# Top-32 attention and expert layer: finding the 32nd largest score from candidates, an exact count and the next eight below

## The chip, the core and the metric

The kernel runs on one NeuronCore of a Trainium2 chip. The time is the device time of one execution in microseconds (us); lower is better. The core has a matrix engine (TensorE, PE in the profile, with its weight loads as PEld), a vector engine (VectorE, DVE), a scalar engine (ScalarE, ACT), a general-purpose engine (GpSimd, POOL) and SyncE (SP), which starts transfers between the memory of the chip (DRAM) and the on-chip buffer SBUF. TensorE writes its results to PSUM. Each engine works through its own list of instructions in order; semaphores order the engines among each other.

## The reference

Everything is float32. Batch 8, 8 heads, 576 positions, head size 64; then 8 experts with 80 places each.

```python
scores = scale * np.matmul(q, k.transpose(0, 1, 3, 2))
kth = np.partition(scores, -top_k, axis=-1)[..., -top_k:-top_k + 1]     # top_k = 32
scores = np.where(scores >= kth, scores, -1000000000.0)
scores = scores - np.max(scores, axis=-1, keepdims=True)
attn = np.exp(scores)
attn = attn / (np.sum(attn, axis=-1, keepdims=True) + 1e-09)
x = np.matmul(attn, v)              # then (B, H, S, D) -> (B*S, H*D) = (4608, 512)
...
logits = x @ w_gate                 # 8 experts: each token goes to the best one
# each expert keeps its 80 tokens with the largest gate weight
h = np.maximum(x[tok_idx] @ w1[e], 0.0)
out[tok_idx] = gate_w[tok_idx, None] * (h @ w2[e])      # all other rows are zero
```

What matters here is `kth`: for each of 8 x 8 x 576 = 36,864 rows of 576 scores the 32nd largest value has to be known exactly, because it decides which scores count.

## The kernel before

The attention works on 32 pairs of heads (four for each batch). A pair has two heads of 576 rows; rows are taken in blocks of 128, so each head has four blocks, and the last 64 rows of both heads share a ninth block. These nine blocks are the **units**; there are 288 in all. A unit is a tile of 128 rows x 576 scores.

A unit goes through these stages:

- `front` (L189, L196): TensorE multiplies q and k into PSUM, ScalarE copies the scores to the SBUF tile `s`.
- `search` (L203 to L209): VectorE finds the 32 largest values of each row, eight at a time. MAX8 gives the eight largest values; match-replace overwrites them in the row by a very low value; three such rounds follow the first MAX8. The 32nd value is the last of `top`.
- `drop` (L216 to L221): `bar` is the 32nd value times 2^90 (GpSimd). ScalarE computes Relu(bar - s * 2^90), which is 0 for a kept score and huge for all others. GpSimd adds the row's maximum and subtracts the sum from the scores: `d`.
- `turn_w` (L229, L231): TensorE transposes `d` in five pieces, ScalarE takes the exponential while it copies the result out of PSUM.
- `back` (L243, L246): TensorE multiplies the weights with v, to which a column of ones is joined, so that the sum of the weights comes out with the product.

After the last unit of a pair `norm` (L257 to L291) divides by that sum on GpSimd, writes x to DRAM and adds to the gate's logits; after two batches `gates` chooses the experts. `turn` (L163 to L165) transposes q and k of the next pair, once in nine units.

The order of all instructions is written out by hand in `step(i)`. One step issues, for VectorE, the first MAX8 of unit i between the rounds of unit i-1 in turn:

```python
for j in range(7):
    if i < NU and j % 2 == 0:
        next(searches[i])
    if 1 <= i <= NU and j % 2:
        next(searches[i - 1])
```

(each `next` is one instruction or one pair), and then `drop(i-1)`, `turn_w(i-2)`, in some steps `turn`, `front` of the units i+2 and i+3, `back(i-2)` and a stage of `norm`. Engines that are ahead simply wait for the data. After the attention the routing finds the 80 best tokens of each expert, and the experts compute (`gather`, `hidden`, `product`, `store`); that part is not changed but for its place in the file.

Of the kernel before, what the change touches and what calls it, by code (L numbers as in the profile page):

```python
# [17 lines left out]
TOP_K = 32  # L18
EPS = 1e-9
LOW = -3.0e38  # L20
BIG = 2.0 ** 90
# [3 lines left out]
def kernel(  # L25
# [32 lines left out]
    GM = 2 * NK  # L58
    FK = F // P

    const = ctx.enter_context(tc.tile_pool(name="const", bufs=1))
    wpool = ctx.enter_context(tc.tile_pool(name="wpool", bufs=4))


    xd = tc.dram_tile([N, Dm], F32, name="xd")

# [8 lines left out]
    tok_i = const.tile([P, NM], I32, name="tok_i")  # L75
    nc.gpsimd.iota(tok_i.rearrange("p (b c) -> p b c", c=NK), pattern=[[S, B], [P, NK]], base=1, channel_multiplier=1)
    tok = const.tile([P, NM], F32, name="tok")
    nc.vector.tensor_copy(tok, tok_i)
    rank_i = const.tile([P, E], I32, name="rank_i")
    nc.gpsimd.iota(rank_i, pattern=[[-1, E]], base=E, channel_multiplier=0)  # L80
    rank = const.tile([P, E], F32, name="rank")
    nc.vector.tensor_copy(rank, rank_i)
# [3 lines left out]
    def load_w(e, parts=1, pool=None):  # L86

        pool = pool or wpool
        w1_t[e] = pool.tile([P, HP, F], F32, name="w1", tag="w1")
        w2_t[e] = pool.tile([P, FK, Dm], F32, name="w2", tag="w2")  # L90
        todo = []
        for t, src, n in ((w1_t[e], moe_w1, HP), (w2_t[e], moe_w2, FK)):
            step = n // parts
            for c in range(0, n, step):
                todo.append(lambda t=t, src=src, c=c, step=step: nc.sync.dma_start(
                    t[:, c : c + step, :],
                    src[e, c * P : (c + step) * P, :].rearrange("(c p) f -> p c f", p=P)))
        return todo

    zrows = 4 * P  # L100
    slow = [lambda i=i: nc.sync.dma_start(
        out[i : i + zrows, :].rearrange("(p r) d -> p r d", p=P),
        zero.unsqueeze(1).to_broadcast([P, zrows // P, Dm])) for i in range(0, N, zrows)]
    for e in range(4):
        slow += load_w(e, 4)


    with ExitStack() as actx:
        nat = actx.enter_context(tc.tile_pool(name="nat", bufs=2))
        qkp = actx.enter_context(tc.tile_pool(name="qkp", bufs=2))  # L110
        rows = actx.enter_context(tc.tile_pool(name="rows", bufs=2))
        small = actx.enter_context(tc.tile_pool(name="small", bufs=3))
        vpool = actx.enter_context(tc.tile_pool(name="vpool", bufs=1))
        ps_s = actx.enter_context(tc.tile_pool(name="ps_s", bufs=2, space=PSUM))
        ps_w = actx.enter_context(tc.tile_pool(name="ps_w", bufs=2, space=PSUM))

        loaded, turned = {}, {}


        NV = 3  # L120
        vb = []
        for j in range(NV):
            t = vpool.tile([CK, NC, 2, D + 1], F32, name=f"vb{j}")
            nc.gpsimd.memset(t[:, :, :, D : D + 1], 1.0)
            nc.gpsimd.memset(t[:DUP, NC - 1, :, :], 0.0)
            vb.append(t)


        xTb = []
        for j in range(2):  # L130
            t = vpool.tile([P, NK * P], F32, name=f"xT{j}")
            nc.gpsimd.memset(t[:, S:], 0.0)
            xTb.append(t)

        def load(n):
            b, hp = divmod(n, HP)
            tiles = []
            for name, src in (("qn", q), ("kn", k)):
                t = nat.tile([P, NK, 2, D], F32, name=name, tag=name, bufs=1)
                for h in range(2):  # L140
                    nc.sync.dma_start(
                        t[:, 0:NF, h, :], src[b, 2 * hp + h, : NF * P, :].rearrange("(c p) d -> p c d", p=P))
                nc.sync.dma_start(
                    t[0:TL, NF, :, :], src[b, 2 * hp : 2 * hp + 2, NF * P :, :].rearrange("h p d -> p h d"))
                tiles.append(t)
            t = vb[n % NV]
            e = (NC - 1) * CK
            for h in range(2):
                nc.sync.dma_start(
                    t[:, : NC - 1, h, :D], v[b, 2 * hp + h, :e, :].rearrange("(c p) d -> p c d", p=CK))  # L150
            nc.sync.dma_start(
                t[DUP:CK, NC - 1, :, :D], v[b, 2 * hp : 2 * hp + 2, e:, :].rearrange("h p d -> p h d"))
            loaded[n] = tiles

        def turn(n):

            ts_ = []
            for i, name in enumerate(("qT", "kT")):
                src = loaded[n][i].rearrange("p c h d -> p c (h d)")
                t = qkp.tile([P, S], F32, name=name, tag=name)  # L160
                ps = ps_w.tile([P, 1024], F32, name="tp", tag="w")
# [5 lines left out]
            turned[n] = ts_  # L167


        units = []  # L170
        for n in range(NP):
            for t in range(NF):
                units += [(n, t, 0), (n, t, 1)]
            units.append((n, NF, 2))
        NU = len(units)
        UPP = NU // NP
        s_t, top_t, d_t, w_t, wT_t, xu_t, xn_t = {}, {}, {}, {}, {}, {}, {}

        def front(n, t):

            qT, kT = turned[n]
            m = P if t < NF else TL
            i = n * UPP + 2 * t
            ps = [ps_s.tile([P, 2, 512], F32, name="sp", tag="sp") for _ in range(2)]
# [6 lines left out]
            for h in range(2):  # L191
                u = i + h if t < NF else i
                if t < NF or h == 0:
                    s_t[u] = rows.tile([P, S], F32, name="s", tag="s", bufs=6)
                o = slice(off[h], off[h] + m)
                nc.scalar.copy(s_t[u][o, :].rearrange("p (j c) -> p j c", j=2), ps[h][o, :, :HS])  # L196

        def search(i):

            s = s_t[i]  # L200
            top = top_t[i] = small.tile([P, TOP_K // 8, 8], F32, name="top", tag="top")
            scr = rows.tile([P, S], F32, name="scr", tag="scr")
            nc.vector.max(out=top[:, 0, :], in_=s)  # L203
            yield
            for r in range(1, TOP_K // 8):
                nc.vector.match_replace(out=scr, in_to_replace=top[:, r - 1, :], in_values=s if r == 1 else scr,  # L206
                                        imm_value=LOW)
                yield
                nc.vector.max(out=top[:, r, :], in_=scr)  # L209
                yield  # L210

        def drop(i):

            s, top = s_t.pop(i), top_t.pop(i)
            bar = small.tile([P, 1], F32, name="bar", tag="bar")
            nc.gpsimd.tensor_scalar(bar, top[:, TOP_K // 8 - 1, 7:8], BIG, None, op0=Alu.mult)  # L216
            low = rows.tile([P, S], F32, name="low", tag="low")
            nc.scalar.activation(low, s, Act.Relu, bias=bar[:, 0:1], scale=-BIG)  # L218
            nc.gpsimd.tensor_scalar(low, low, top[:, 0, 0:1], 1.0, op0=Alu.add, op1=Alu.mult)  # L219
            d_t[i] = rows.tile([P, S], F32, name="d", tag="d")  # L220
            nc.gpsimd.tensor_tensor(out=d_t[i], in0=s, in1=low, op=Alu.subtract)  # L221

        def turn_w(i):

            dd = d_t.pop(i)
            w_t[i] = ps_w.tile([P, 1024], F32, name="pw", tag="w")
            for c in range(NC):
                k0 = c * CK if c < NC - 1 else S - CK
                nc.tensor.transpose(w_t[i][:CK, c * P : (c + 1) * P], dd[:, k0 : k0 + CK], ident)  # L229
            wT_t[i] = rows.tile([CK, NC, P], F32, name="wT", tag="wT")  # L230
            nc.scalar.activation(wT_t[i].rearrange("p c r -> p (c r)"), w_t[i][:CK, : NC * P], Act.Exp, scale=scale)  # L231

        def back(i):
            n, t, h = units[i]
            wT, pw = wT_t.pop(i), w_t.pop(i)
            if t == 0 and h == 0:
                xu_t[n] = rows.tile([P, NK, 2, D + 1], F32, name="xu", tag="xu")
            xu = xu_t[n]
# [3 lines left out]
            for c, (j, hh, r, p) in order:  # L242
                nc.tensor.matmul(pw[p : p + TL, o + j * (D + 1) : o + (j + 1) * (D + 1)], lhsT=wT[:, c, r : r + TL],  # L243
                                 rhs=vb[n % NV][:, c, hh, :], start=(c == 0), stop=(c == NC - 1))
# [5 lines left out]
        def norm(n):  # L250

            xu = xu_t.pop(n)
            xn_t[n] = rows.tile([P, NK, 2, D], F32, name="xn", tag="xn", bufs=1)
            parts = ((slice(0, P), slice(0, NF)), (slice(0, TL), slice(NF, NK)))
            z = small.tile([P, NK, 2], F32, name="z", tag="z")
# [6 lines left out]
            for p, cs in parts:  # L262
                nc.gpsimd.tensor_tensor(out=xn_t[n][p, cs, :, :], in0=xu[p, cs, :, :D], op=Alu.mult,  # L263
                                        in1=z[p, cs, :].unsqueeze(3).to_broadcast([p.stop, cs.stop - cs.start, 2, D]))
            b, hp = divmod(n, HP)
            xn = xn_t.pop(n).rearrange("p c h d -> p c (h d)")
            cols = slice(hp * P, (hp + 1) * P)
            nc.sync.dma_start(xd[b * S : b * S + NF * P, cols].rearrange("(c p) d -> p c d", p=P), xn[:, :NF, :])
            nc.sync.dma_start(xd[b * S + NF * P : (b + 1) * S, cols], xn[:TL, NF, :])
            yield  # L270
            yield
            ps = ps_w.tile([P, 1024], F32, name="tp", tag="w")
# [3 lines left out]
            xT = xTb[n % 2]  # L276
            nc.scalar.copy(xT[:, :S], ps[:, :S])
            yield
            ps = ps_w.tile([P, 1024], F32, name="tp", tag="w")
# [3 lines left out]
            if b % 2 == 0 and hp == 0:  # L283
                lg_t[b // 2] = small.tile([P, 2, NK, E], F32, name="lg", tag="lg", bufs=2)
            lg = lg_t[b // 2][:, b % 2]
            if hp == 0:
                nc.scalar.copy(lg, lp)
            else:
                part = small.tile([P, NK, E], F32, name="part", tag="part", bufs=2)
                nc.scalar.copy(part, lp)  # L290
                nc.gpsimd.tensor_tensor(out=lg, in0=lg, in1=part, op=Alu.add)  # L291
            if (n + 1) % (2 * HP) == 0:
                yield
                yield from gates(b // 2)

        lg_t = {}

        def gates(g):

# [289 lines left out]
```

## Time and profile before

| | |
|---|---|
| time, median of 3 runs | 1612.83 us (1612.36 to 1612.85) |
| span of the profiled run | 1611.3 us |
| VectorE busy | 1459.1 us (91%) |
| TensorE matmul busy | 1126.3 us (70%) |
| GpSimd busy | 770.0 us (48%) |
| ScalarE busy | 710.4 us (44%) |
| mean TensorE clock | 0.739 of full speed |
| first search begins, last search ends | 11.34 us, 1431.85 us |

A row of the page's groups has the line and engine, the operation, output <- input with partitions x elements and how often it ran; then the busy time of the group and the mean duration of one in ns; then how long its engine had been idle just before such instructions, and what ended most of that idle time. A row of the timeline has start, duration, engine, line and the same names. The durations of neighbours on one engine can overlap: the pace of an engine is read from the distance of the starts.

### The profile page before, as it was taken

What the parts mean: (1) busy time and instruction counts of PE and PEld (TensorE: products, weight loads), DVE (VectorE), ACT (ScalarE), POOL (GpSimd) and SP (SyncE); (2) the same over time, 40 slices, a digit from 0 to 9 for tenths busy, and PEclk for the clock granted to TensorE, in tenths of its full rate; (3) what the DMA queues carried; (4) which work ended last, traced back from release to release, by engine and by line L of the source; (5) the groups of instructions that cost most, each with busy time, mean ns of one, the idle gap of its engine ahead of it and who ended that gap; (6) DMA issues with size and microseconds to landing.
All of it is one profiled execution on the core that took longest, in us unless ns stands there. A gap on an engine that the chain in (4) does not pass through costs nothing. (4 is left out here: it accounts for less than half of the span.)

```text
span 1611.3 us, 30682 instructions
## 1 busy us (share of the span) xinstructions
PE 1126.3 (70%) x11501; PEld 836.2 (52%) x11501; DVE 1459.1 (91%) x3075; ACT 710.4 (44%) x1341; POOL 770.0 (48%) x1071
## 2 busy tenths in 40 slices
PE   4777777676677767767766777677667777760688
PEld 3455545555455555555555555555555555540687
DVE  7999999999999999999999999999999999968311
ACT  3444454444454444545444544545454455430011
POOL 3455555555554555555555555555555555540111
PEclk9777777777777777777677777777777777765699
DMA  3022222221112222222111121111111000011280
GB/s 93 1 82 83 82 83 56 56 57 40 39 35 57 56 56 57 56 56 57 47 47 35 42 56 30 31 30 31 31 31 31 24 19 19 9 52 68 74 288 23
DMA packets 153267, 85.35 MB, mean 53 GB/s; under 512 B 117024, under 2 KB 135456, under 8 KB 153120
## 3 DMA queue, kind: packets, MB, share of 16 engines
q1 hardware_dynamic: 152096, 80.78, 18.6%
q0 software_dynamic: 1024, 2.62, 0.5%
q8 instruction: 91, 1.49, 0.4%
q14 instruction: 56, 0.46, 0.1%
HBM read 63.19 MB, written 20.19 MB: 52 GB/s over the span
## 5 line engine op out<-in xcount | busy, mean ns | idle before, releaser
L209 DVE MAX8 top<-scr 128x8 f32<-128x576 f32 x864 | 620.7, 746 | 0.1
L243 PE MATMUL pw<-vb,wT 116*64 116x65 f32 x5760 | 314.0, 262 | 267.8 <-ACT wT L231 265.3
L243 PEld LDWEIGHTS pw<-vb,wT 116*64 116x64 f32 x5760 | 267.5, 170 | 408.3 <-ACT wT L231 385.3
L206 DVE MATCH_REPLACE8 scr<-top,scr 128x576 f32<-128x576 f32 x576 | 428.1, 743 | 0.0
L221 POOL TENSOR_TENSOR d<-s,low 128x576 f32<-128x576 f32 x288 | 406.3, 1411 | 24.0
L218 ACT ACTIVATE low<-s,bar 128x576 f32<-128x576 f32 x288 | 223.6, 776 | 402.3 <-POOL bar L216 402.3
L229 PE MATMUL pw<-ident,d 128*116 128x128 f32 x1440 | 305.2, 362 | 108.2 <-POOL d L221 103.8
L219 POOL TENSOR_SCALAR low<-low,top 128x576 f32<-128x576 f32 x288 | 214.7, 745 | 313.8 <-ACT low L218 293.0
L189 PE MATMUL sp<-kT,qT 64*128 64x288 f32 (+1 forms) x1280 | 295.4, 593 | 1.4 <-ACT kT L165 0.7
L229 PEld LDWEIGHTS pw<-ident,d 128*116 128x116 f32 x1440 | 215.1, 179 | 147.0 <-POOL d L221 141.7
L203 DVE MAX8 top<-s 128x8 f32<-128x576 f32 x288 | 216.5, 752 | 28.1 <-ACT s L196 28.1
L196 ACT COPY s<-sp 128x576 f32<-128x576 f32 (+1 forms) x320 | 191.2, 640 | 73.7 <-PE sp L189 72.6
L216 POOL TENSOR_SCALAR bar<-top 128x1 f32<-128x1 f32 x288 | 61.4, 213 | 327.0 <-DVE top L209 323.3
L206 DVE MATCH_REPLACE8 scr<-top,s 128x576 f32<-128x576 f32 x288 | 214.0, 743 | 0.0
L231 ACT ACTIVATE wT<-pw 116x640 f32<-116x640 f32 x288 | 197.5, 686 | 8.6 <-PE pw L229 8.5
L189 PEld LDWEIGHTS sp<-kT,qT 64*128 64x128 f32 (+1 forms) x1280 | 152.4, 247 | 69.8 <-issue 48.7
L246 ACT COPY xu<-pw 128x65 f32<-128x65 f32 x256 | 56.2, 219 | 120.9 <-PE pw L243 114.4
L163 PE MATMUL tp<-ident,kn 128*128 128x128 f32 x128 | 33.4, 411 | 37.1 <-ACT qT L165 36.5
L533 DVE TENSOR_SCALAR y<-yx,a 80x512 f32<-80x512 f32 x8 | 6.0, 747 | 44.2 <-PE yx L531 44.2
L206 DVE MATCH_VALUE_LOAD scr<-top,scr 128x8 f32 x576 | 44.8, 78 | 0.1
L534 POOL DMA_INDIRECT out_dram<-y,idx_s x8 | 7.4, 929 | 78.3 <-DVE y L533 78.3
L263 POOL TENSOR_TENSOR xn<-xu,z 128x512 f32<-128x512 f32 x64 | 44.6, 719 | 0.1
(147 smaller groups left out, 660.0 us busy)
## 6 DMA issues: line engine op xcount, KB each, us to landing
w<-in_moe_w_dram SPq DMA_DIRECT2D x32, 512.0 KB
w<-in_moe_w_dram SPq DMA_DIRECT2D x8, 2048.0 KB
out_dram<-zero SPq DMA_DIRECT2D x9, 1024.0 KB
qn<-in_q_dram SPq DMA_DIRECT2D x64, 128.0 KB
kn<-in_k_dram SPq DMA_DIRECT2D x64, 128.0 KB
xd<-xn SPq DMA_DIRECT2D x32, 256.0 KB
vb<-in_v_dram SPq DMA_DIRECT2D x64, 116.0 KB
vb<-in_v_dram SPq DMA_DIRECT2D x32, 56.0 KB
```

The costliest lines, as they stand in the source:

```text
L189: nc.tensor.matmul(ps[h][off[h] : off[h] + m, j, :HS], lhsT=qT[d, t * P : t * P + m], rhs=kT[d, j * HS : (j + 1) * HS], start=True, stop=True)
L196: nc.scalar.copy(s_t[u][o, :].rearrange("p (j c) -> p j c", j=2), ps[h][o, :, :HS])
L203: nc.vector.max(out=top[:, 0, :], in_=s)
L206: nc.vector.match_replace(out=scr, in_to_replace=top[:, r - 1, :], in_values=s if r == 1 else scr, imm_value=LOW)
L209: nc.vector.max(out=top[:, r, :], in_=scr)
L216: nc.gpsimd.tensor_scalar(bar, top[:, TOP_K // 8 - 1, 7:8], BIG, None, op0=Alu.mult)
L218: nc.scalar.activation(low, s, Act.Relu, bias=bar[:, 0:1], scale=-BIG)
L219: nc.gpsimd.tensor_scalar(low, low, top[:, 0, 0:1], 1.0, op0=Alu.add, op1=Alu.mult)
L221: nc.gpsimd.tensor_tensor(out=d_t[i], in0=s, in1=low, op=Alu.subtract)
L229: nc.tensor.transpose(w_t[i][:CK, c * P : (c + 1) * P], dd[:, k0 : k0 + CK], ident)
L231: nc.scalar.activation(wT_t[i].rearrange("p c r -> p (c r)"), w_t[i][:CK, : NC * P], Act.Exp, scale=scale)
L243: nc.tensor.matmul(pw[p : p + TL, o + j * (D + 1) : o + (j + 1) * (D + 1)], lhsT=wT[:, c, r : r + TL], rhs=vb[n % NV][:, c, hh, :], start= ...
```

## The change

The full search is replaced by a shorter one that doesn't always succeed, with a count that tells whether it did:

1. `parts`: the row is cut into six parts of 96 scores, and MAX8 gives the eight largest of each: 48 candidates.
2. `search`: MAX8 and match-replace over the 48 candidates give their 24th largest value, `w9[7]`.
3. One instruction over the whole row makes `y = (s >= w9[7]) - s` and sums it into `cnt`. The scores have been scaled by 2^-48 when they were copied from PSUM, so that in float32 the sum is exactly the number of scores that are at least `w9[7]`, and `y` is 1 for those and -s for the others.
4. `turn_sign`: GpSimd negates `y`; MAX8 over it gives the next eight values below, `w9[8:]`.
5. `pick`: with the count between 24 and 32, the 32nd largest value is one of the nine values `w9[7:]`; a comparison of the count with the numbers 32 to 24, multiplied by these values and summed, picks it.

A row whose count is not between 24 and 32 makes the result useless. `judge` looks for such a row in all counts after the attention, and at the end of the program a branch on every engine runs the whole kernel again with the full search if there is one. `bar` is gone, since the scaled scores can be subtracted first and multiplied by 2^100 afterwards. A unit now takes part in three steps of the search: `drop` comes at i-3, `turn_w` and `back` at i-4, and there are 7 tiles `s` in place of 6.

```diff
-                nc.scalar.copy(s_t[u][o, :].rearrange("p (j c) -> p j c", j=2), ps[h][o, :, :HS])
+                nc.scalar.activation(self.s[u][o, :].rearrange("p (j c) -> p j c", j=2), ps[h][o, :, :HS], Act.Copy,
+                                     scale=TINY)
...
-            nc.vector.max(out=top[:, 0, :], in_=s)
-            yield
-            for r in range(1, TOP_K // 8):
-                nc.vector.match_replace(out=scr, in_to_replace=top[:, r - 1, :], in_values=s if r == 1 else scr,
-                                        imm_value=LOW)
-                yield
-                nc.vector.max(out=top[:, r, :], in_=scr)
-                yield
+        def parts(self, i):
...
+            for j in range(NG):
+                nc.vector.max(out=cand[:, j, :], in_=s[:, j * S // NG : (j + 1) * S // NG])
+                yield
...
+        def search(self, i):
...
+            for r in range(G0 // 8):
+                dst = top[:, r, :] if r < G0 // 8 - 1 else w9[:, :8]
+                nc.vector.max(out=dst, in_=cand)
+                yield
+                if r < G0 // 8 - 1:
+                    nc.vector.match_replace(out=cand, in_to_replace=dst, in_values=cand, imm_value=LOW)
+                    yield
+            y = self.y[i] = self.rows.tile([P, S], F32, name="y", tag="y")
+            nc.vector.scalar_tensor_tensor(out=y, in0=s, scalar=w9[:, 7:8], in1=s, op0=Alu.is_ge, op1=Alu.subtract,
+                                           accum_out=self.cnt[:, i : i + 1])
+            yield
+            nc.vector.max(out=w9[:, 8:], in_=self.y.pop(i))
+            yield
...
+            nc.vector.scalar_tensor_tensor(out=pick, in0=past, scalar=self.cnt[:, i : i + 1], in1=w9[:, 7:], accum_out=self.thr[i],
+                                           op0=Alu.is_equal, op1=Alu.mult)
+            yield
...
+        def turn_sign(self, i):
+            y = self.y[i]
+            nc.gpsimd.tensor_scalar(y, y, -1.0, 0.0, op0=Alu.mult, op1=Alu.add)
...
-            nc.gpsimd.tensor_scalar(bar, top[:, TOP_K // 8 - 1, 7:8], BIG, None, op0=Alu.mult)
...
-            nc.scalar.activation(low, s, Act.Relu, bias=bar[:, 0:1], scale=-BIG)
-            nc.gpsimd.tensor_scalar(low, low, top[:, 0, 0:1], 1.0, op0=Alu.add, op1=Alu.mult)
+            nc.scalar.activation(low, s, Act.Relu, bias=thr[:, 0:1], scale=-1.0)
+            nc.gpsimd.tensor_scalar(low, low, BIG, top[:, 0, 0:1], op0=Alu.mult, op1=Alu.add)
...
+                for c in "GbGcGdGeGgGfah":
+                    if c == "G":
+                        if i < NU:
+                            next(first[i])
+                    elif c == "a":
+                        if i < NU:
+                            next(first[i], None)
+                            second[i] = self.search(i)
+                            next(second[i])
+                    elif i - (2 if c in "gh" else 1) in second:
+                        next(second[i - (2 if c in "gh" else 1)])
+                if 0 <= i - 3 < NU:
+                    self.drop(i - 3)
+                if 0 <= i - 1 < NU:
+                    self.turn_sign(i - 1)
+                if 0 <= i - 4 < NU:
+                    self.turn_w(i - 4)
...
+            att.run(slow)
+            att.judge()
+        finish(wpool)
+    with tc.If(nc.values_load(bad[0:1, 0:1]) > 0):
+        for dma in clear():
+            dma()
```

In the string `GbGcGdGeGgGfah`, which is the order on VectorE within a step, `G` is a part of unit i; `a` to `e` are the three MAX8 and two match-replaces over the candidates (`a` of unit i, `b` to `e` of unit i-1); `f` is the count of unit i-1; `g` is the MAX8 of `y` and `h` the pick, both of unit i-2.

## The prediction, as it was put on record

> **What bounds the kernel now.** I read the page's busy shares first, then its groups of instructions, then a stretch of the timeline from mid-run.
>
> ```profile
> PE 1126.3 (70%) x11501; PEld 836.2 (52%) x11501; DVE 1459.1 (91%) x3075; ACT 710.4 (44%) x1341; POOL 770.0 (48%) x1071
> ...
> L209 DVE MAX8 top<-scr 128x8 f32<-128x576 f32 x864 | 620.7, 746 | 0.1
> ...
> L221 POOL TENSOR_TENSOR d<-s,low 128x576 f32<-128x576 f32 x288 | 406.3, 1411 | 24.0
> L218 ACT ACTIVATE low<-s,bar 128x576 f32<-128x576 f32 x288 | 223.6, 776 | 402.3 <-POOL bar L216 402.3
> ...
> L219 POOL TENSOR_SCALAR low<-low,top 128x576 f32<-128x576 f32 x288 | 214.7, 745 | 313.8 <-ACT low L218 293.0
> ```
>
> DVE is full and idles 0.1 us in front of its largest group; the 402 us in which ScalarE waits come from DVE through `bar`. So the search sets the pace. The timeline of DVE gives that pace:
>
> ```profile
> 700.28 0.08 DVE L206 MATCH_VALUE_LOAD scr<-top,scr 128x8 f32 x1
> 700.34 0.75 DVE L206 MATCH_REPLACE8 scr<-top,scr 128x576 f32<-128x576 f32 x1
> 701.00 0.75 DVE L203 MAX8 top<-s 128x8 f32<-128x576 f32 x1
> 701.66 0.75 DVE L209 MAX8 top<-scr 128x8 f32<-128x576 f32 x1
> ...
> 705.10 0.08 DVE L206 MATCH_VALUE_LOAD scr<-top,scr 128x8 f32 x1
> ```
>
> From 700.28 to 705.10 is one unit: 4.82 us. Starts are 0.66 us apart although each instruction lasts 0.75, so independent neighbours overlap. 576 elements in 0.66 us and 8 elements in 0.065 us fit a fixed 0.06 us plus one element per 1.04 ns. 288 units at 4.82 us are 1388 us; the first search starts at 11.34 us and the last ends at 1431.85 us. The remaining 179.5 us (last weighting, routing, experts) are outside the search.
>
> [...] The search of before has one input everywhere, so only the four gatings touch this. Two of them show it:
>
> ```profile
> 770.43 0.24 DVE L312 TENSOR_TENSOR oh<-oh,mx 128x80 f32<-128x80 f32 x1
> 770.47 0.82 POOL L219 TENSOR_SCALAR low<-low,top 128x576 f32<-128x576 f32 x1 [0.91 <-ACT low L218]
> ```
>
> POOL's instruction lasts 0.82 us in place of its 0.745 median, because an 80-element two-input DVE instruction (83 ns of elements) began 0.04 us earlier. The trace agrees for POOL as the loser; DVE as the loser it doesn't show. [...] L309 (80 fp32 elements) lasts 234 ns beside 241 ns of a tensor-tensor of that size. It has no accumulator, though, so I keep half rate for the range. [...] the same five transposes take 0.76 or 1.32 us, mean clock 0.73.
>
> **The change, part by part.**
>
> DVE, per unit. Removed: 4 MAX8 and 3 match-replaces of 576, 3 value loads: 4.82 us. Added, by the law above: six MAX8 of 96 at 0.16 = 0.96; three of 48 at 0.11 = 0.33; two match-replaces of 48 with loads at 0.175 = 0.35; the count (scalar-tensor-tensor of 576) 0.66; MAX8 of 576 0.66; the pick of 9 elements 0.07. Both accumulating instructions may carry a separate accumulator read, which no row of before shows: between 0 and 0.2 us each; I take a value load's 0.065. Sum 3.16 us. Dependent neighbours are kept apart by another unit's part: 0.27 us from start to start where a 48-element result takes about 0.24, so no stall. DVE falls by 1.66 us, 478 us over 288 units. I don't expect all of it, since other engines close in.
>
> POOL, per unit. Added: the sign turn of 128x576, a tensor-scalar like L219: 0.745 busy, 0.83 from start to start. Removed: `bar` (0.21). `low` (0.83) and `d` (1.37 start to start) stay. The normalisation per head pair, L257, L263 and L291, is 0.48 + 1.44 + 0.20 = 2.1 us, or 0.24 per unit. POOL's own work is 0.83 + 0.83 + 1.37 + 0.24 = 3.27 us: above DVE.
>
> The lock. The count reads two SBUF tensors, and POOL is now nearly always reading SBUF. Take the count's start as 0. It and its read end at 0.725, the next unit's first MAX8 at 0.835, the pick's threshold lands at 1.0 (a tiny DVE instruction, L465, lasts 172 ns). ScalarE's Relu follows after 0.03 and takes 0.78: 1.81. `low` starts 0.09 later, at 1.90, `d` at 2.73, and ends at 4.14. The sign turn ran in between, 0.73 to 1.5. DVE meanwhile issues 5 parts (0.80), 2 replaces (0.35), 2 small MAX8 (0.22), the MAX8 of `y` (0.66) and a sixth part (0.16) and wants its next count at 3.16, when `d` holds the port since 2.73. It waits until 4.14: **pitch 4.15 us**, DVE idle for 1 us. Queued behind the count on DVE are the pick, whose threshold Relu and then POOL wait for, so the loop closes on itself. If a delay lets the count slip in between `low` and `d`, POOL runs without gaps: 0.83 + 0.83 + 1.37 and some 0.62 in which the count blocks it, 3.65, plus 0.24: **pitch 3.89 us**. Both states are possible, the normalisation steps push into the second.
>
> The step that also transposes q and k. On TensorE it takes 8.3 us (688.41 to 696.67), and ScalarE does the copies behind it before the next Relu. Before, that cost DVE 0.9 us per head pair (L203's 28.1 us), because DVE waits for nothing else. Now DVE's MAX8 of `y` waits for the sign turn, which queues behind `low` and `d`, which wait for that Relu. The Relu comes 2 to 4 us late, of which about 1 us is slack: 1 to 3 us in nine units, 0.1 to 0.35 each. I add 0.2 to 3.89 and nothing to 4.15, which has idle time on DVE and POOL to catch up: pitch 4.1 us.
>
> TensorE, the same work: 140.8 us busy in 200 us, about 30.7 per head pair, with some 7 us of waits for the exponential, is 37.7 us per nine units, or 4.2 each, at clock 0.73. That is no slack, but at a shorter pitch it is busier and the clock should rise: at 0.8 it is 3.9.
>
> At no cost: copies out of PSUM that scale (the same pass over 576 elements on ScalarE, which has 2.5 us of work per unit); s in 7 buffers; `judge`, a few DVE instructions, beside the drain of the last units; two steps more of pipeline, one of them chained, 2.7 us from last count to last pick. The branch at the end: a load of `bad` and a jump on each engine, partly beside the landing of the last scatter: 1 to 5 us, I take 2. The second copy of the kernel doesn't run: with the seeded inputs in float32 the count lies between 24 and 32 in all 36,864 rows (34,596 at 24, one at 32).
>
> Sum: first count at about 15.5 us (11.34, one step, half the next), 287 pitches, 2.7, 179.5, 2: 200 + 287 x 4.1 = **1377 us**.
>
> **The rivals.**
> 1. No lock on DVE's side: the count slips by. POOL 3.27 and TensorE at a warmer clock 3.6 set the pitch; at 3.5, 200 + 1005 = 1205 us. For it: before shows no DVE instruction held up. Against: POOL was.
> 2. TensorE and ScalarE bound: the clock stays near 0.7, the transposing step adds its full 0.35 to 4.15: 4.5, 1492 us. For it: 4.2 us of TensorE chain. Against: the clock's rise with activity.
> 3. The count at half rate (0.6 us more, all in the loop): 4.75, 1563 us.
> 4. Slower than before: half rate and the transposing step's 0.35 together, 5.1, 1664 us; or a row counted over 32 on the chip, which runs everything again, far above 2000 us.
>
> **How the numbers follow.** Forecast (pitch 3.9 to 4.3, 1320 to 1434 us) 0.55; no lock 0.18, spread over 1150 to 1260; TensorE 0.15; half rate 0.08; slower 0.04. The range 1200 to 1510 leaves out about a third of the no-lock case, half rate and slower: 0.18. Faster: all but the last, 0.95; the same 0.01.
>
> **What would show it.** DVE's busy share falls to some 70%, with idle time or a lengthened duration at the count, overlapping `d` on POOL; MAX8 of 96 start 0.16 us apart; POOL is 75 to 85% busy; the clock rises over 0.74; the tail is still 180 us. Counts of 0.75 us that overlap `d` would refute the lock; counts that always last 1.3 us, whether or not POOL is reading, would mean half rate; TensorE without gaps in the search would mean rival 2.

## The result, and the profile after

| | before | after |
|---|---|---|
| time, median of 4 runs | 1612.84 us (1612.36 to 1614.19) | 1469.88 us (1466.17 to 1474.09) |
| ratio, 95% interval | | 0.9113 (0.9086 to 0.9141) |
| span of the profiled run | 1611.3 us | 1469.7 us |
| mean from count to count (before: from first MAX8 to first MAX8) | 4.92 us | 4.41 us |
| mean TensorE clock | 0.739 | 0.780 |

The change saves 143 us, 9%; the forecast was 236 us. The page's line of busy times:

```profile
PE 1068.7 (73%) x11502; PEld 799.3 (54%) x11502; DVE 1241.3 (84%) x5385; ACT 721.5 (49%) x1341; POOL 961.4 (65%) x1072
```

VectorE is busy for 218 us less, and POOL for 191 us more. The instruction counts are those of one pass (TensorE has 11502 instead of 11501), so the full search didn't run. But 1241 us can't all be work. By the forecast's sum VectorE needs 3.16 us per unit, 910 us for 288 units, and about 60 us in the stretch after the last pick. The rest, more than 200 us, must lie inside instructions that last longer than their work. The groups of the page show which:

```profile
L253 POOL TENSOR_TENSOR d<-s,low 128x576 f32<-128x576 f32 x288 | 459.5, 1596 | 24.0
...
L251 POOL TENSOR_SCALAR low<-low,top 128x576 f32<-128x576 f32 x288 | 223.5, 776 | 208.8 <-ACT low L250 184.7
L219 DVE SCALAR_TENSOR_TENSOR y<-s,w 128x576 f32<-128x576 f32 x288 | 347.7, 1207 | 0.0
...
L222 DVE MAX8 w<-y 128x8 f32<-128x576 f32 x288 | 213.3, 741 | 86.4 <-POOL y L232 86.4
...
L226 DVE SCALAR_TENSOR_TENSOR pick<-past,cnt,w 128x9 f32<-128x9 f32 x288 | 183.6, 638 | 0.1
```

The pick (L226) works on nine elements and has a mean of 638 ns. The count (L219) has 1207 ns, while a MAX8 over as many elements (L222) has 741. A mean can hide two populations, so the next view is the durations, as min/median/max in ns, from the rows of the trace's answers on these three lines:

```profile
L219 DVE SCALAR_TENSOR_TENSOR y<-s,w x288: 790/1209/1971, 13.8 to 1279.4; 128x576 f32<-128x576 f32 x144
...
L226 DVE SCALAR_TENSOR_TENSOR pick<-past,cnt,w x288: 201/209/1244, 17.7 to 1283.9; 128x9 f32<-128x9 f32 x144
...
L253 POOL TENSOR_TENSOR d<-s,low x288: 1397/1407/2042, 21.5 to 1289.0; 128x576 f32<-128x576 f32 x144
```

Undisturbed, the count takes 0.79 us, the pick 0.20 and `d` 1.40. Over the 288 units the counts are 120 us longer than their minimum, the picks 125 us, and `d` 55 us (each a sum of duration minus an undisturbed 0.79, 0.205 or 1.405 us). No idle time in front of an instruction shows any of this; it lies inside the instructions, and so counts as busy. It follows what runs on the other engine. The 120 counts that began while `d` ran lasted 1.08 to 1.97 us and ended 0.60 to 0.62 us after `d`; the 113 picks that did lasted 1.23 to 1.24 us and ended 0.02 to 0.04 us after it; the 100 counts and 151 picks that began while POOL ran nothing lasted at most 0.90 and 0.23 us. The other way round, the 113 `d` that began while a count ran lasted 1.77 to 2.04 us and ended 1.24 to 1.27 us after the count; the other 175 lasted at most 1.42. These waits are what is called the lock here. Some recorded texts speak of a port; the traces show the waits, not what is behind them.

The timeline shows two states. In the first, VectorE's count starts while `d` runs:

```profile
641.38 1.41 POOL L253 TENSOR_TENSOR d<-s,low 128x576 f32<-128x576 f32 x1
...
641.71 1.69 DVE L219 SCALAR_TENSOR_TENSOR y<-s,w 128x576 f32<-128x576 f32 x1
...
643.46 0.20 DVE L226 SCALAR_TENSOR_TENSOR pick<-past,cnt,w 128x9 f32<-128x9 f32 x1
643.50 0.70 POOL L232 TENSOR_SCALAR y<-y 128x576 f32<-128x576 f32 x1 [0.71 <-DVE y L219]
...
645.64 0.23 DVE L202 MAX8 cand<-s 128x8 f32<-128x96 f32 x1
645.80 1.63 DVE L219 SCALAR_TENSOR_TENSOR y<-s,w 128x576 f32<-128x576 f32 x1
```

`d` ends at 642.79, and the count, begun at 641.71, ends at 643.40: 1.08 us of wait, then a little over 0.6 us of work. The next count follows after 4.09 us. Counts wait behind `low` as well, though it reads only one SBUF tensor (here 1.21 us in place of 0.79):

```profile
632.90 0.74 POOL L251 TENSOR_SCALAR low<-low,top 128x576 f32<-128x576 f32 x1
633.04 1.21 DVE L219 SCALAR_TENSOR_TENSOR y<-s,w 128x576 f32<-128x576 f32 x1
```

Of the 169 counts that lasted over 0.9 us, 120 began while `d` ran and 49 while `low` ran; of the 135 picks over 0.3 us, 113 and 22 (these 0.49 to 0.70 us). The waits behind `low` are short: they make up 25 of the 245 us. In the second state the count is first:

```profile
658.52 0.76 DVE L222 MAX8 w<-y 128x8 f32<-128x576 f32 x1 [2.16 <-POOL y L232]
658.62 0.75 POOL L251 TENSOR_SCALAR low<-low,top 128x576 f32<-128x576 f32 x1
...
659.36 0.80 DVE L219 SCALAR_TENSOR_TENSOR y<-s,w 128x576 f32<-128x576 f32 x1
659.45 1.97 POOL L253 TENSOR_TENSOR d<-s,low 128x576 f32<-128x576 f32 x1
...
660.21 1.24 DVE L226 SCALAR_TENSOR_TENSOR pick<-past,cnt,w 128x9 f32<-128x9 f32 x1
```

Now `d` waits for the count (1.97 us in place of 1.40), and then the pick, which also reads two SBUF tensors (`past` and `w9`), waits until `d` ends at 661.42 (1.24 us in place of 0.20). The threshold comes a microsecond late for ScalarE's Relu, and VectorE has stood still behind nine elements. Sorted by state over the 277 units after the first ten, with the transposing steps apart, the distances from count to count average 4.07 us where only the count waits (116 units), 4.32 us where only the pick waits (80), 4.54 us where both wait (48), and 5.79 us in the steps that transpose q and k (31); in the other two units neither waits. Below, a step's position is the number of the unit in its pair, 0 to 8, from whose count it runs to the next count; the transposing step is position 2. The 2.16 us in brackets at 658.52 belong to such a step: VectorE idles because the sign turn is late.

### The profile page after: what moved, and what is told of

Read it like the earlier page. It is cut to its first block, busy times and chain, and to the rows that moved or that the text cites. A ratio compares the mean times of both kernels' runs of the same rounds, so it can differ in the third digit from the quotient of the medians.

```text
span 1469.7 us, 32849 instructions
## 1 busy us (share of the span) xinstructions
PE 1068.7 (73%) x11502; PEld 799.3 (54%) x11502; DVE 1241.3 (84%) x5385; ACT 721.5 (49%) x1341; POOL 961.4 (65%) x1072
## 4 chain that ended last, share of the span: by engine, by line
DVE 58%; POOL 15%; PE 14%; issue 10%; ACT 1%; DMA 0%; SPq 0%; POOLq 0%; DVEq 0%; ACTq 0%
DVE y L219 18%; DVE cand L202 12%; DVE w L222 9%; DVE pick L226 8%; POOL d L253 7%; DVE cand L216 4%; POOL low L251 4%; POOL y L232 4%; DVE top L213 3%; PE yp L603 3%; PE sp L187 2%; PE pw L275 2%; PE pw L261 2%; DVE w L213 1%; DVE top L478 1%
## 5 line engine op out<-in xcount | busy, mean ns | idle before, releaser
L202 DVE MAX8 cand<-s 128x8 f32<-128x96 f32 x1728 | 416.4, 241 | 12.9 <-ACT s L194 12.9
L219 DVE SCALAR_TENSOR_TENSOR y<-s,w 128x576 f32<-128x576 f32 x288 | 347.7, 1207 | 0.0
L250 ACT ACTIVATE low<-s,thr 128x576 f32<-128x576 f32 x288 | 223.9, 777 | 129.2 <-DVE pick L226 126.5
L222 DVE MAX8 w<-y 128x8 f32<-128x576 f32 x288 | 213.3, 741 | 86.4 <-POOL y L232 86.4
L232 POOL TENSOR_SCALAR y<-y 128x576 f32<-128x576 f32 x288 | 196.6, 683 | 98.8 <-DVE y L219 98.8
L194 ACT ACTIVATE s<-sp 128x576 f32<-128x576 f32 (+1 forms) x320 | 193.7, 648 | 129.2 <-PE sp L187 128.2
L226 DVE SCALAR_TENSOR_TENSOR pick<-past,cnt,w 128x9 f32<-128x9 f32 x288 | 183.6, 638 | 0.1
L213 DVE MAX8 top<-cand 128x8 f32<-128x48 f32 x576 | 111.5, 194 | 0.1
L216 DVE MATCH_REPLACE8 cand<-top,cand 128x48 f32<-128x48 f32 x576 | 107.2, 186 | 0.0
L213 DVE MAX8 w<-cand 128x8 f32<-128x48 f32 x288 | 53.8, 187 | 0.0
```

The source lines that it names most:

```text
L202: nc.vector.max(out=cand[:, j, :], in_=s[:, j * S // NG : (j + 1) * S // NG])
L213: nc.vector.max(out=dst, in_=cand)
L219: nc.vector.scalar_tensor_tensor(out=y, in0=s, scalar=w9[:, 7:8], in1=s, op0=Alu.is_ge, op1=Alu.subtract, accum_out=self.cnt[:, i : i + 1])
L222: nc.vector.max(out=w9[:, 8:], in_=self.y.pop(i))
L226: nc.vector.scalar_tensor_tensor(out=pick, in0=past, scalar=self.cnt[:, i : i + 1], in1=w9[:, 7:], accum_out=self.thr[i], op0=Alu.is_equal ...
L232: nc.gpsimd.tensor_scalar(y, y, -1.0, 0.0, op0=Alu.mult, op1=Alu.add)
```

## The experiments

The theory after the comparison (A) is that two separate things keep the kernel at 4.41 us: the lock between VectorE's two-input instructions and POOL, the pick included, and the transposing step, whose delay of the Relu now reaches VectorE through the sign turn. The rival (B) is that the amount of work on another engine, POOL or TensorE with ScalarE, sets the time and the waits only fill it up. In all twelve kernels the time from the first count to the last, less the waits of counts and picks and VectorE's idle time, is 3.21 to 3.32 us per unit. So a change helps by what the two kinds of waiting, in the lock and idle, lose together; several experiments below only turn one into the other. Medians of 4 runs each; the ratio is to the kernel before, run on the same chip:

| kernel | us | ratio, 95% interval |
|---|---|---|
| after | 1469.88 | 0.9086 to 0.9141 |
| pick with one SBUF input | 1444.73 | 0.8943 to 0.8997 |
| count and pick with one input | 1378.82 | 0.8532 to 0.8588 |
| q and k transposed in two steps | 1434.79 | 0.8882 to 0.8922 |
| no sign turn on POOL | 1417.94 | 0.8747 to 0.8840 |
| one input each, two steps | 1278.53 | 0.7889 to 0.7959 |
| pick before count, two steps | 1426.68 | 0.8806 to 0.8858 |
| earlier count, two steps | 1374.24 | 0.8461 to 0.8534 |
| pick with one input, two steps | 1396.06 | 0.8638 to 0.8682 |
| earlier count alone | 1414.98 | 0.8744 to 0.8835 |
| one input each, two steps, short normalisation | 1231.62 | 0.7620 to 0.7646 |
| earlier count, two steps, short normalisation | 1328.13 | 0.8217 to 0.8268 |

### The pick's second input

```diff
-            nc.vector.scalar_tensor_tensor(out=pick, in0=past, scalar=self.cnt[:, i : i + 1], in1=w9[:, 7:], accum_out=self.thr[i],
-                                           op0=Alu.is_equal, op1=Alu.mult)
+            nc.vector.tensor_scalar(pick, w9[:, 7:], self.cnt[:, i : i + 1], 0.0, op0=Alu.is_equal, op1=Alu.add,
+                                    accum_out=self.thr[i])
```

> Changed kernel, but the pick reads one SBUF tensor instead of two (a comparison of the nine values with the count, summed; the multiplication is left out, so thresholds are not the real ones). Theory A ([...] the pick alone waits 125 us in all): the pick always lasts about 0.2 us, and the time falls by 30 to 120 us, to 1350 to 1440. Theory B (TensorE and ScalarE set the pitch and VectorE's waits only fill its idle time): the picks are short, but other waits grow by as much, and the time stays within 15 us of 1470.

Measured: 1444.73 us, 25 us less: outside both forecasts, though only just short of theory A's. Groups of this kernel's page:

```profile
L253 POOL TENSOR_TENSOR d<-s,low 128x576 f32<-128x576 f32 x288 | 499.0, 1733 | 24.0
...
L222 DVE MAX8 w<-y 128x8 f32<-128x576 f32 x288 | 219.1, 761 | 234.1 <-POOL y L232 234.1
...
L226 DVE TENSOR_SCALAR_CACHE_REDUCE pick<-w,cnt 128x9 f32<-128x9 f32 x288 | 58.9, 205 | 0.1
```

All picks take 0.2 us now: the 125 us are gone from the picks (205 ns on average in place of 638): with one SBUF input they do not wait. But the time falls by a fifth of that. An undisturbed unit takes 3.57 us, while the transposing step goes from 5.79 to 6.99 us, and VectorE's wait for the sign turn from 86 to 234 us; `d` loses 94 us to counts in place of 55. A shorter loop reaches the late Relu sooner and waits longer for it.

### No second input in the count either

```diff
-            nc.vector.scalar_tensor_tensor(out=y, in0=s, scalar=w9[:, 7:8], in1=s, op0=Alu.is_ge, op1=Alu.subtract,
-                                           accum_out=self.cnt[:, i : i + 1])
+            nc.vector.tensor_scalar(y, s, w9[:, 7:8], 0.0, op0=Alu.is_ge, op1=Alu.add, accum_out=self.cnt[:, i : i + 1])
```

(with the pick's edit above)

> As before, and the count too reads one SBUF tensor (the comparison alone, summed; minus s is left out, so y holds only zeros and ones). No VectorE instruction of the search then has two SBUF tensors. Theory A: count about 0.8 us and pick 0.2 us always, d on GpSimd 1.41 us always; the pitch goes to GpSimd's own 3.3 us plus what the transposing step costs, 1210 to 1300 us. Theory B: above 1420 us.

Measured: 1378.82 us, 91 us less than after, between the two forecasts. No instruction of the search waits in the lock any more: count 0.80, pick 0.21, `d` 1.41 us in all nine positions of a pair. Undisturbed units come 3.17 us apart, which is VectorE's own work as the forecast summed it (3.16). The transposing step takes 7.10 us, which theory A had not reckoned with. The timeline around one:

```profile
644.09 0.20 DVE L225 TENSOR_SCALAR_CACHE_REDUCE pick<-w,cnt 128x9 f32<-128x9 f32 x1
...
644.97 2.38 PE L187 MATMUL sp<-kT,qT 64*128 64x288 f32 x8
645.37 0.64 ACT L173 COPY kT<-tp 128x576 f32<-128x576 f32 x1 [1.50 <-PE tp L172]
...
647.39 1.19 ACT L194 ACTIVATE s<-sp 128x576 f32<-128x576 f32 x2 [1.39 <-PE sp L187]
...
648.88 0.77 ACT L249 ACTIVATE low<-s,thr 128x576 f32<-128x576 f32 x1
...
649.74 0.75 POOL L250 TENSOR_SCALAR low<-low,top 128x576 f32<-128x576 f32 x1 [4.94 <-ACT low L249]
...
651.94 0.67 POOL L231 TENSOR_SCALAR y<-y 128x576 f32<-128x576 f32 x1
652.64 0.76 DVE L221 MAX8 w<-y 128x8 f32<-128x576 f32 x1 [1.61 <-POOL y L231]
```

The threshold is there at 644.3, but the Relu that needs it stands in ScalarE's list behind the copies of qT and kT and of two score tiles, which wait for TensorE, and starts at 648.88. POOL stands for 4.94 us; the sign turn is queued behind `low` and `d`, and VectorE waits for the sign turn. This is the whole way from the transposes to VectorE. One thing more lies on it, TensorE's clock: the eight matmuls of the scores at 644.97 take 2.38 us, and in 24 of 30 pairs 2.26 to 2.38; from 644.9 to 648.6 the granted clock is 0.54. In the six pairs in which they took 1.29 us the transposing step averages 5.47 us, in the 24 others 7.62. In after it is 4.78 us in two pairs and 5.93 in 28. So a good part of what this step costs goes with the slow scores and the low clock; no run changes the clock alone.

### The transposes in two steps

q is transposed in the fourth step of a pair and k in the sixth, in place of both in the third; `turn` is told which of the two to do. The kernel computes everything.

```diff
...
-                    if t == 1 and h == 0 and n + 1 < NP:
-                        self.turn(n + 1)
+                    if t in (1, 2) and h == 1 and n + 1 < NP:
+                        self.turn(n + 1, (t - 1,))
```

> Changed kernel, but the transposes of q and of k for the next pair go to two steps of their own, in which no scores are computed. The step with both now lasts 5.8 us from count to count instead of about 4.2. Theory A: that excess of 1.5 us in each of 31 pairs goes, the other steps stay: 1420 to 1445 us. Theory B: ScalarE and TensorE are relieved as well, so all steps shorten: below 1400 us. If the excess is only moved to other steps: 1470 us.

Measured: 1434.79 us, 35 us less, in theory A's band. The position of the old transposing step falls from 5.79 to 4.23 us, about as long as its neighbours; 31 times 1.56 us is 48 us, of which 35 arrive. Picks and counts wait about as before (121 and 138 us), so the gain does not come from the lock. The two new steps compute no scores, so this run does not tell whether the parting of the transposes or their move helps.

### No sign turn on POOL

VectorE's MAX8 reads `s` in place of the turned `y`, and `turn_sign` is gone.

```diff
-            nc.vector.max(out=w9[:, 8:], in_=self.y.pop(i))
+            nc.vector.max(out=w9[:, 8:], in_=s)
...
-                if 0 <= i - 1 < NU:
-                    self.turn_sign(i - 1)
```

> Changed kernel without the sign turn on GpSimd; the MAX8 that read y reads s instead (so the next eight values are not the real ones). GpSimd has 0.75 us less per unit and VectorE no longer waits for it (86 us). Theory A: the count still meets d, since nothing moves them apart; only the wait for the sign turn goes: 1370 to 1430 us. Theory C (GpSimd's amount of work sets the pitch): 288 x 0.75 = 215 us less, about 1255 us.

Measured: 1417.94 us, in theory A's band. POOL lost 177 us of work (961.4 to 784.7 busy) and the kernel 52 us: POOL's amount of work isn't what sets the time. The transposing step still took 6.57 us, with VectorE now waiting for the scores from ScalarE (105 us in front of L202 in place of 13), and counts and picks still waited 65 and 86 us.

### Both causes at once

The edits of the second and the third experiment together.

> e2 and e3 together: no VectorE instruction of the search has two SBUF tensors (the count without minus s, the pick without the multiplication), and the transposes of q and k lie in two steps. Theory A (two causes besides VectorE's own work: the lock, and the transposing step, whose Relu waits behind ScalarE's copies): what remains is VectorE's 3.16 us and, in the steps of the normalisation, GpSimd: pitch 3.3 to 3.7, 1150 to 1270 us. Theory B (TensorE's amount of work sets the pitch once the lock is gone): above 1320 us. In e2 the steps with nothing special had a pitch of 3.17 us and the transposing step 7.1 us.

Measured: 1278.53 us, slightly above theory A's band and below theory B's. One-input instructions alone gave 91 us, the split alone 35, both 191. That is more than the sum; in the single experiments VectorE's other waits had grown or stayed. TensorE's granted clock rose to 0.853, so the amount of TensorE's work, the same throughout, was no floor at 1470 us. What is left lies in the normalisation steps (positions 6, 8 and 0), at 4.1 to 4.3 us against 3.17 to 3.5 for plain units, and at position 2, at 4.64 us, although q and k are no longer transposed there: the steps that their copies now delay, positions 3 and 5, take 3.25 and 3.18 us. The short normalisation, the last experiment, throws light on both.

### The pick before the count

In VectorE's order the pick goes ahead of the count (with the transposes in two steps):

```diff
-                for c in "GbGcGdGeGgGfah":
+                for c in "GbGcGdGeGgGhfa":
```

> e3, and in each step the pick goes in front of the count (order GbGcGdGeGgGhfa). All of the computation is there. Theory A: the pick no longer loses the port to the d that waited for the count (121 us of waiting in e3), and its threshold leaves VectorE one count earlier, so that Relu, low and d start earlier: 1330 to 1400 us. If the count then waits for d as long as both did before: 1435 us as e3.

Measured: 1426.68 us, a miss. Groups of this kernel's page:

```profile
L219 DVE SCALAR_TENSOR_TENSOR y<-s,w 128x576 f32<-128x576 f32 x288 | 383.2, 1331 | 0.0
...
L222 DVE MAX8 w<-y 128x8 f32<-128x576 f32 x288 | 214.8, 746 | 99.5 <-POOL y L232 99.5
...
L226 DVE SCALAR_TENSOR_TENSOR pick<-past,cnt,w 128x9 f32<-128x9 f32 x288 | 99.7, 346 | 0.1
```

The picks' wait falls from 121 us to 41, and the counts' rises from 138 to 156: together 63 us less in the lock. But VectorE's idle time in front of the MAX8 of `y` rises from 40.0 to 99.5 us and takes nearly all of it back. What the picks no longer wait in the lock, VectorE waits for the sign turn.

### The earlier count

The count moves ahead of the MAX8 of `y` in VectorE's order:

```diff
-                for c in "GbGcGdGeGgGfah":
+                for c in "GbGcGdGeGfGgah":
```

First with the transposes in two steps:

> e3, and in each step the count goes in front of the MAX8 of y and a part (order GbGcGdGeGfGgah). All of the computation is there. Theory A: the count asks for the port 0.8 us earlier, while low runs on GpSimd and before d starts, so it waits less; but the pick then asks while d runs and waits up to 1.2 us: 1370 to 1440 us. If only the order of waits changes: 1435 us as e3.

Measured: 1374.24 us, in theory A's band, with the computation complete, and the best such kernel here: 96 us faster than after, 239 us than before. The counts' wait is 76 us, the picks' 64, that of `d` 26. Counts still wait, 190 of them, but 105 now begin while the sign turn runs, and these wait 0.44 us on average, against 0.86 behind `d` with the transposes in two steps alone. Then the order alone:

> Only the order written out by hand changes: the MAX8 of the next unit's turned scores (g) moves one DVE instruction later, behind the count (f) of the unit after it, so the count leaves DVE earlier in the unit. Theory A (the count loses the port to d because it comes late in the unit; the transposing step is a separate cost of about 35 us, as undoing it alone showed): 1395 to 1425 us. Theory B (the earlier count helps only once the transposing step is split): above 1450 us.

Measured: 1414.98 us, in theory A's band: 55 us less than after. With the 35 us of the split this makes 90; together they gave 96: within the spread of the runs these two effects add.

### The pick with one input, and the transposes in two steps

The edits of the first and the third experiment together.

> e1 and e3 together (pick with one SBUF tensor, its multiplication left out; transposes in two steps). Theory A: in e1 the plain steps had a pitch of 3.57 us and the transposing step 7.0 us, which ate the gain; without that step 9 units take about 35 us: 1290 to 1350 us. Theory B: within 20 us of e3's 1435 us.

Measured: 1396.06 us, a miss on the size: 39 us less than the split alone, where the picks had waited 121 us. The plain units reach 3.57 to 3.75 us, the steps at positions 0, 2, 6 and 8 stay at 4.45 to 4.95 and position 4 at 4.0. With the picks free, `d` still waits for counts (80 us over its minimum), and VectorE's idle time in front of the MAX8 of `y` rises from 40 to 208 us.

### The short normalisation

The multiplication by 1/z on POOL reaches 8 of 64 columns of a tile that is set to one at the start:

```diff
...
-                nc.gpsimd.tensor_tensor(out=xn[p, cs, :, :], in0=xu[p, cs, :, :D], op=Alu.mult,
-                                        in1=z[p, cs, :].unsqueeze(3).to_broadcast([p.stop, cs.stop - cs.start, 2, D]))
+                nc.gpsimd.tensor_tensor(out=xn[p, cs, :, :8], in0=xu[p, cs, :, :8], op=Alu.mult,
+                                        in1=z[p, cs, :].unsqueeze(3).to_broadcast([p.stop, cs.stop - cs.start, 2, 8]))
```

> The kernel with one-input count and pick and the transposes in two steps, whose multiplication by 1/z on POOL is done for 8 of 64 columns (the others are left at one; the pick's multiplication is left out as before). POOL loses about 1.2 us per head pair, 40 us in all. Theory A (what is left over the 3.2 us of VectorE's own work is the normalisation on POOL, which stands in the loop of sign, low and d): from 1278 down to 1190 to 1240 us, the step with the multiplication near 3.3. Theory B (TensorE's and ScalarE's extra work in those steps sets them): 1260 to 1280 us.

> The kernel with the count earlier in the order and the transposes in two steps, whose multiplication by 1/z on POOL is done for 8 of 64 columns (the others are left at one). Theory A (POOL's normalisation pushes the loop into the state in which d and the count meet): 1374 down to 1300 to 1345 us. Theory B (the two-input instructions meet d anyway): 1350 to 1375 us.

Measured: 1231.62 us and 1328.13 us, both in theory A's band, 47 and 46 us less than the same kernels with the whole multiplication. In the kernel without the lock VectorE's wait for the sign turn, from the groups of its page, is

```profile
L223 DVE MAX8 w<-y 128x8 f32<-128x576 f32 x288 | 217.0, 754 | 88.2 <-POOL y L233 85.9
```

against 129.5 us with the whole multiplication, and the step at position 6 goes from 4.23 to 3.59 us. The 30 us that POOL's multiplication lost (44.5 to 14.9 busy) came back as 47, which fits a multiplication that stands in the loop of sign turn, `low`, `d` and the next Relu. From count to count this kernel takes 3.575 us: where the first rival of the prediction had put a kernel without the lock (3.5).

In the kernel with the lock the band was met, but not by theory A's way. The waits of counts, picks and `d` grew from 167 us (76, 64 and 26) to 248 (64, 120 and 64), so the meetings cost more than before; what fell is VectorE's idle time in front of the MAX8 of `y`, from 99 to 9 us.

Position 2 still takes 4.57 us in the kernel without the lock. Its timeline shows why, here from 373.57 (count) to 378.55 (next count):

```profile
370.19 2.29 PE L189 MATMUL sp<-kT,qT 64*128 64x288 f32 x8
372.51 1.19 ACT L196 ACTIVATE s<-sp 128x576 f32<-128x576 f32 x2 [1.45 <-PE sp L189]
...
373.92 0.78 ACT L251 ACTIVATE low<-s,thr 128x576 f32<-128x576 f32 x1
...
374.78 0.60 PE L174 MATMUL tp<-ident,qn 128*128 128x128 f32 x4
374.79 0.75 POOL L252 TENSOR_SCALAR low<-low,top 128x576 f32<-128x576 f32 x1 [2.29 <-ACT low L251]
...
377.00 0.68 POOL L233 TENSOR_SCALAR y<-y 128x576 f32<-128x576 f32 x1
377.70 0.76 DVE L223 MAX8 w<-y 128x8 f32<-128x576 f32 x1 [1.69 <-POOL y L233]
```

The Relu waits behind two score tiles that come late from TensorE, and it has begun before q is transposed, as in all 29 pairs from the third on: it isn't the transposes that hold this step. One pair earlier the same matmuls took 1.24 us in place of 2.29, and the step took 3.18 us with q's transposes in it:

```profile
336.81 1.24 PE L189 MATMUL sp<-kT,qT 64*128 64x288 f32 x8
```

So it is in two of 30 pairs; in the 25 in which these matmuls took over 2.2 us the step averages 4.71 us. This is a comparison within one run, without a run that sets the clock, but it points to the slow scores at this place as what is left. In after, from 30 us on, eight such matmuls took 1.19 to 1.29 us in the 74 stretches with a granted clock of 1.00, and 2.18 to 2.38 us in the 51 with 0.50.

## Why the prediction was right, and where it was short

**The bound and its shift: right.** VectorE's work fell to 3.16 us per unit as summed (3.17 measured without the lock). The instruction after a part's MAX8 starts 0.16 us later (645.64 to 645.80), as priced. POOL was put above VectorE at 3.27, normalisation included; without the lock and outside the normalisation units come at VectorE's own 3.17 us, and the sign turn takes 0.67 us, not 0.745. VectorE's busy share is 84% instead of the 70% named as a sign, as its waits count as busy; POOL's is 65% instead of 75 to 85. The accumulator's read was put at 0.065 us: from an undisturbed count's start to the next instruction's start it is 0.73 us (653.91 to 654.64), where 576 elements without an accumulator take 0.66 (653.09 to 653.75, a MAX8 of `y`). The read has rows of its own in after, of 0.07 to 0.09 us each behind count and pick:

```profile
653.91 0.79 DVE L219 SCALAR_TENSOR_TENSOR y<-s,w 128x576 f32<-128x576 f32 x1
654.64 0.08 DVE L219 DVE_READ_ACCUMULATOR y<-s,w 128x1 f32 x1
```

The full search did not run.

**Half rate: refuted, as the prediction leaned.** An undisturbed count takes 790 ns with its accumulator. Half rate was an assumption with no trace behind it, and by the prediction's estimate would have made it 0.6 us longer. A one-input instruction with an accumulator in its place takes 795 ns, so the second input costs a scalar-tensor-tensor of 576 fp32 elements nothing here. L309, which the prediction weighs against half rate, is such an instruction with 80 elements.

**The lock: right, with the state it described.** In before it showed on POOL alone, and not twice but three times: three of 288 `low` (L219) lasted 0.82 us, each begun 0.04 us after an L312, and the others 0.74 to 0.75. VectorE as the loser, which before didn't show, is the count of 1.69 us that began 0.33 us after `d`. The state was put at 4.15 us and measured at 4.07. Both sides lose, with the same shapes: 169 counts and 113 of the `d` waited (over 0.9 and 1.6 us), each time the one that began later.

**The first step that fell short: the pick was left out of the lock.** The sum priced the pick at 0.07 us of VectorE, and the second state at 3.89 us, with only the count and `d` against each other. The pick has two SBUF inputs too and follows the count, just when `d` runs. That state costs 4.32 us, and 4.54 with both waits. At the measured mix of states (116 units and 128) the forecast's 4.15 and 3.89 give a plain unit of 4.01 us; measured are 4.25. That is 0.24 us per unit, some 69 us of the 93 that were missing. This is a sum, not an experiment: taking the pick's wait away gave 25 us alone and 39 with the transposes in two steps, as other waits grew.

**The second: the transposing step.** The delay of 1 to 3 us in nine units was foreseen, with its way through Relu, `low` and sign turn; but 0.2 per unit was added to the fast state alone and nothing to the other, for "idle time on DVE and POOL to catch up". At the measured mix that makes 0.10 us per unit. The step costs 1.54 us more than a plain unit, once in nine, 0.17 us per unit, and nothing is caught up: the two steps after it take 4.31 and 4.36 us, as long as other plain ones. So 0.07 us per unit were missing, some 20 us. With the first this makes 0.31 us, times 287 units 89 us. Moving the transposes to two steps gave 35 of the 48 us back that the step costs in all. The forecast reckoned with a mean clock; that the clock is mostly low in this very step it left out (in 28 of 30 pairs of after the scores took 2.2 us or more, at a granted clock of 0.50 to 0.55).

**The tail: 4 us short.** First count at 13.8 (15.5 assumed), last count to last pick 4.4 us (2.7), last pick to end 185.8 (181.5, of which 2 were a guess for the branch). Three units' weights still follow the last pick. 89 and 4 are the 93 us between 1377 and the profiled 1469.7.

**The rivals, and luck.** TensorE as the bound (1492) is nearest in time, but wrong in the main: it put the transposing step at 0.35 us per unit (measured 0.17) and the clock near 0.7 (0.780), and TensorE, with the same work, ran in a kernel of 1278 us at a clock of 0.853. The clock was higher at the shorter pitch, as forecast: 0.739 before, 0.780 after, 0.853 in the kernel of 1278 us and 0.879 in that of 1232. In the last slices of after's page it goes with TensorE's busy share too: 0.5 where the share is 0.3 and 0.1, in the 36th and 37th, and 0.9 where it is 0.8 and 0.7, in the last two:

```profile
PE   6677777777777777777777777787777777631887
...
PEclk8888877887788787787877778777887778755799
```

Which of them leads, no run separates. The forecast's own band of 1320 to 1434 us was missed. That the time lies within the range is in part luck: the range reached up to 1510 for this rival, not for the waits of the pick.

## What to carry to other kernels

Before adding a VectorE instruction with two SBUF inputs next to a GpSimd stream, count every such instruction, however small: the price of the pick's nine elements here was 0.20 us, or 1.24 where it met a `d` of 1.40 us, and the wait counted as busy. Compare a group's mean with the minimum of the same shape; the gap was the wait (638 ns against 201 for the pick). Add up waits of this kind and idle time before calling a wait removed: in three experiments here one in part became the other. And where a change closes a loop over several engines in order, look for the step that comes late in it, and place instructions by what the other engine runs when they start (with the transposes in two steps, counts waited 0.86 us on average behind `d`, and in the earlier order 0.44 where they began during the sign turn), before buying speed in any single engine.

## What the runs showed of the hardware beyond expectation

- A VectorE instruction of 128 x 9 elements with two SBUF inputs takes from 0.20 to 1.24 us beside GpSimd's tensor-tensor of 1.40 us; with one input, the comparison alone, it takes 0.20 to 0.22 us in the kernel with one input each, two steps and short normalisation.
- A GpSimd tensor-scalar that reads one SBUF tensor makes such instructions wait too: counts that began while `low` (0.745 us) ran took up to 1.24 us, and picks up to 0.70.
- The loser isn't always the same: the count lasted up to 1.97 us where `d` had begun first, and `d` up to 2.04 us where the count had.
- The same eight matmuls of scores took 1.19 to 1.29 us at a granted clock of 1.00 in after, and 2.18 to 2.38 at 0.50; in the kernel with one input each, 2.38 in a stretch with a clock of 0.54 (644.9 to 648.6).
